# Sign-paired key features with 65-column key-value products, and the last 96 gate and up columns computed token-major and turned by a crossbar transpose

## The chip, the cores and the metric

The kernel runs on one NeuronCore of a Trainium2 chip (trn2). The metric is the device time of one execution in microseconds (us), the median of several. "Idle" always means idle time of TensorE unless another engine is named. The span of a profile is about 1.7 us shorter than the time of the same execution; both are given where they are used, and not mixed.

## The reference, cut to what matters

The input has S = 2048 tokens of D = 512 values. Two blocks, a linear attention (A) and a gated layer (B), run twice: A, B, A, B. In what follows "first attention" and "second attention" are the two A blocks, B1 and B3 the two gated layers.

```python
def A(x, wqkv, w_phi, wo):                    # 32 heads of 16
    q, k, v = split(x @ wqkv)                 # per head
    pq, pk = q @ w_phi, k @ w_phi             # per head, 16x16
    phi_q = concat([softmax(pq), softmax(-pq)])   # two signs of 16 features
    phi_k = concat([softmax(pk), softmax(-pk)])
    kv  = einsum("bhsf,bhsd->bhfd", phi_k, v) # sum over all 2048 tokens
    z   = einsum("bhsf->bhf", phi_k)
    num = phi_q @ kv ;  den = phi_q @ z + 1e-6
    return concat_heads(num / den) @ wo

def B(x, W_gate, W_up, W_down):               # F = 1376 = 10*128 + 96
    return (relu(x @ W_gate) * (x @ W_up)) @ W_down

x = x + A(layernorm(x)); x = x + B(layernorm(x))
x = x + A(layernorm(x)); x = x + B(layernorm(x))
```

## The kernel before, the parts that matter

The program is a list of operations, each with what it reads and writes, a declared duration and a name. A list scheduler inside the kernel orders them per engine from the declared durations, before anything runs. So a change of one operation changes the order of all.

`phik` scales the exponentials of the keys by their row sums (the softmax). `kv_acc` adds one token tile to the key-value sums: 8 products per tile, 16 tiles, each the 128 features of eight heads of one sign against the 128 values of the same eight heads. Only the eight diagonal blocks of 16x16 are wanted, so 7/8 of each product is thrown away. One more column, the 129th, is all ones and gives z. `kv_fin` masks the diagonal blocks out of PSUM into `kvbd`, a bank at a time, and `num` multiplies it with the queries' features.

```python
def knorm(self, t, tag):          # softmax of the key features of tile t
    op("dve", ... tensor_reduce(Zk, expk[:, t] as (s h) x 16), ...)           # row sums
    op("dve", ... reciprocal(rZk, Zk), ...)
    parts = [("pool", 0, 2)] if t < NT - 2 else [("pool", 0, 1), ("dve", 1, 2)]
    for eng, s0, s1 in parts:
        op(eng, ... tensor_tensor(expk, expk, rZk broadcast, ALU.mult), ..., f"{tag} phik {t} {s0}")

def kv_acc(self, t, tag):
    for g in range(NG):                                # 8 groups: 2 signs x 4 blocks of 8 heads
        s, c = g // 4, g % 4
        bank, j = g // 3, g % 3                        # three PSUM banks
        op("pe", ... matmul(pb[bank][:, j*130 : j*130+129],
                            expk[:, t, s, c*128:(c+1)*128], vsb[:, t, c, 0:129],
                            start=(t == 0 and j == 0), stop=(t == NT-1)),
           [r("phik", t, s), r("v", t), r("vones")], [RP[bank]], 59, f"{tag} kvacc {t} {g}")

def kv_fin(self, tag):
    for bank in range(3):                              # waits for ONE bank
        op("dve", ... tensor_tensor(kvbd[:, g0:g0+n, 0:128], pv[:, :, 0:128], mask8, ALU.mult),
           [RP[bank], r("mask8")], [r("kvbd", bank)], ...)
        op("dve", ... scalar_tensor_tensor(kvbd[:, g0:g0+n, 128:136], pv[:, :, 128:129], ...), ...)

def num(self, t, ...):                                 # needs kvbd of its bank only
    op("pe", ... matmul(pb[bank], expq[...], kvbd[:, g0 + j, :]), [r("expq", ...), r("kvbd", gb), ...], ...)
    # ... evacuate, divide, then a crossbar transpose of the result and the product with wo:
    dma_tr(... dma_start_transpose(oT[:, ob], osb[:, b]), ..., f"{tag} otr {t}")

def glu_up(self, ts, ...):                             # 128 rows of F at a time, feature-major
    def step(fc):
        Mf = 128 if fc < 10 else FLAST                 # FLAST = 96
        for bank, W in ((gb, Wg), (ub, Wu)):
            for ic in range(4):
                op("pe", ... matmul(pb[bank][0:Mf, 0:n], W[:, ic, fc*128 : fc*128+Mf], yT[:, ic, c0:c0+n]), ...)
        # relu on ACT, product on DVE into hT
```

In most stages the layer norm's result reaches TensorE through a crossbar transpose too, `tr t`, from `ytile` to `yT`.

The softmax here doesn't subtract the row's maximum and nothing guards it: scores larger than these inputs give would overflow.

Of the kernel before, what the change touches and what calls it, by code (L numbers as in the profile page):

```python
# [347 lines left out]
ALU = mybir.AluOpType  # L348
ACT = mybir.ActivationFunctionType
AX = mybir.AxisListType  # L350
P = 128

S, D, H, DH, F = 2048, 512, 32, 16, 1376
# [5 lines left out]
EPS_LN = 1e-5  # L359
EPS_DEN = 1e-6  # L360

WINDOW = {"sp": 24, "act": 64, "pe": 400, "dve": 40, "pool": 24}
# [6 lines left out]
class Kernel:  # L369
# [27 lines left out]
    def alloc(self, E):  # L397
        nc = self.nc

        def sb(name, shape, dt=BF16):  # L400
            t = E(nc.sbuf_tensor(name, [P] + shape, dt))
            setattr(self, name, t)
            return t

        sb("x_sb", [NT, 512])
        sb("yT", [NC, S])
        sb("wv_p", [NC, 512])
        sb("Wqp", [NC, 512])
        sb("Wkp", [NC, 512])
        sb("wo_p", [NC, 512])  # L410
        sb("Wg", [NC, F])
        sb("Wu", [NC, F])
        sb("Wd", [NFC, 512])
        sb("expk", [NT, 2, 512])
        sb("vsb", [NT, NC, 130])
        sb("expq", [NSLAB, NC, 2, 512])
        sb("kvbd", [NG, GW])
        sb("hT", [NHU, 512])
        sb("numbf", [2, NG, GW])
        sb("tsc", [2, 1024])  # L420
        sb("osb", [2, 512])
        sb("oT", [4, NC, 128])
        sb("gate_sb", [3, 512])
        sb("ytile", [4, 512])
        sb("ident", [128])
        sb("mask8", [8])
        sb("mask8t", [8])
        sb("phi_c", [NC, DH])
        sb("stats6", [NT, 6], FP32)
        sb("mv", [NT, 2], FP32)  # L430
        sb("rv1", [NT, 1], FP32)
        sb("rstd", [NT, 1], FP32)
        sb("nmr", [NT, 1], FP32)
        sb("agg", [4, 3], FP32)
        sb("aggw", [2], FP32)
        sb("mhalf", [4, 1], FP32)
        sb("Zk", [2, 64], FP32)
        sb("rZk", [4, 64], FP32)
        sb("zm", [2, 64], FP32)
        sb("zd", [2, 32], FP32)  # L440
        sb("zr", [2, 32], FP32)
        sb("ab", [2, 64])
        self.ps = E(nc.psum_tensor("ps", [P, 8, 512], FP32))
        self.pb = [self.ps[:, i, :] for i in range(8)]
        self.RP = [self.r("pb", i) for i in range(8)]


    def setup(self):
# [47 lines left out]
        op("pool", lambda e: e.memset(k.aggw[:, 1:2], 1.0 / D), [], [r("aggw")], 100, "agg w1")  # L496
        op("pool", lambda e: e.memset(k.vsb[:, :, :, 128:130], 1.0), [], [r("vones")], 250, "v ones")
        op("pool", lambda e: e.tensor_copy(k.kvbd[:, :, 136:144], k.mask8[:].unsqueeze(1).to_broadcast([P, NG, 8])), [r("mask8")], [r("kvones")], 230, "kv ones")
# [113 lines left out]
    def kv_proj(self, t, ring, tag):  # L612
# [6 lines left out]
        for s in range(2):  # L619
            op("act", (lambda s: lambda e: e.activation(k.expk[:, t, s, :], k.pb[bk][:], ACT.Exp, scale=(1.0 - 2.0 * s)))(s),  # L620
               [self.RP[bk]], [r("expk", t, s)], 605, f"{tag} expk {t} {s}")
        op("act", lambda e: e.activation(k.vsb[:, t, :, 0:128], k.pb[bv][:].rearrange("p (c n) -> p c n", c=4), ACT.Copy),
           [self.RP[bv]], [r("v", t)], 600, f"{tag} vcopy {t}")
        self.knorm(t, tag)

    def knorm(self, t, tag):
        op, r, k = self.op, self.r, self
        zb, rb = t % 2, t % 4
        op("dve", lambda e: e.tensor_reduce(k.Zk[:, zb, :], k.expk[:, t, :, :].rearrange("p s (h f) -> p (s h) f", f=16), AX.X, ALU.add),  # L629
           [r("expk", t, 0), r("expk", t, 1)], [r("Zk", zb)], 1215, f"{tag} Zk {t}")  # L630
        op("dve", lambda e: e.reciprocal(k.rZk[:, rb, :], k.Zk[:, zb, :]), [r("Zk", zb)], [r("rZk", rb)], 545, f"{tag} rZk {t}")  # L631
        parts = [("pool", 0, 2)] if t < NT - 2 else [("pool", 0, 1), ("dve", 1, 2)]
        for eng, s0, s1 in parts:
            op(eng, (lambda s0, s1: lambda e: e.tensor_tensor(  # L634
                k.expk[:, t, s0:s1, :].rearrange("p s (h f) -> p (s h) f", f=16),
                k.expk[:, t, s0:s1, :].rearrange("p s (h f) -> p (s h) f", f=16),
                k.rZk[:, rb, s0 * 32:s1 * 32].unsqueeze(2).to_broadcast([P, (s1 - s0) * 32, 16]), ALU.mult))(s0, s1),
               [r("expk", t, s) for s in range(s0, s1)] + [r("rZk", rb)], [r("phik", t, s) for s in range(s0, s1)],
               (1930 if s1 - s0 == 2 else 980) if eng == "pool" else 1050, f"{tag} phik {t} {s0}")

    def kv_pair(self, t, ring, tag):
# [8 lines left out]
        for s in range(2):  # L650
            op("act", (lambda s: lambda e: e.activation(k.expk[:, t:t + 2, s, :], k.ps[:, kb[0]:kb[0] + 2, :], ACT.Exp, scale=(1.0 - 2.0 * s)))(s),
               [self.RP[b] for b in kb], [r("expk", tt, s) for tt in ts], 1030, f"{tag} expk {t} {s}")
        op("act", lambda e: e.activation(k.vsb[:, t:t + 2, :, 0:128], k.ps[:, vb[0]:vb[0] + 2, :].rearrange("p b (c n) -> p b c n", c=4), ACT.Copy),
           [self.RP[b] for b in vb], [r("v", tt) for tt in ts], 1030, f"{tag} vcopy {t}")
# [3 lines left out]
    def kv_acc(self, t, tag):  # L658
        op, r, k = self.op, self.r, self
        for g in range(NG):  # L660
            s, c = g // 4, g % 4
            bank, j = g // 3, g % 3
            op("pe", (lambda s, c, bank, j: lambda e: e.matmul(  # L663
                k.pb[bank][:, j * 130:j * 130 + 129], k.expk[:, t, s, c * 128:(c + 1) * 128], k.vsb[:, t, c, 0:129],
                start=(t == 0 and j == 0), stop=(t == NT - 1), skip_group_check=True))(s, c, bank, j),
               [r("phik", t, s), r("v", t), r("vones")], [self.RP[bank]], 59, f"{tag} kvacc {t} {g}")

    def kv_fin(self, tag):
        op, r, k = self.op, self.r, self
        for bank in range(3):  # L670
            g0 = bank * 3
            n = min(3, NG - g0)
            pv = k.pb[bank][:, 0:n * 130].rearrange("p (g m) -> p g m", m=130)
            op("dve", (lambda g0, n, pv: lambda e: e.tensor_tensor(
                k.kvbd[:, g0:g0 + n, 0:128].rearrange("p g (d h) -> p g d h", h=8),
                pv[:, :, 0:128].rearrange("p g (h d) -> p g d h", h=8),
                k.mask8[:].unsqueeze(1).unsqueeze(1).to_broadcast([P, n, 16, 8]), ALU.mult))(g0, n, pv),
               [self.RP[bank], r("mask8")], [r("kvbd", bank)], 550 if n == 3 else 430, f"{tag} kvbd {bank}")
            op("dve", (lambda g0, n, pv: lambda e: e.scalar_tensor_tensor(
                k.kvbd[:, g0:g0 + n, 128:136], pv[:, :, 128:129].to_broadcast([P, n, 8]), 0.5 * EPS_DEN,  # L680
                k.mask8[:].unsqueeze(1).to_broadcast([P, n, 8]), ALU.add, ALU.mult))(g0, n, pv),
               [self.RP[bank], r("mask8"), r("kvbd", bank)], [r("kvbd", bank)], 200, f"{tag} kvden {bank}")

# [12 lines left out]
    def num(self, t, nring, wring, tag):  # L696
# [3 lines left out]
        for gb in range(3):  # L700
# [3 lines left out]
            for j in range(n):  # L704
# [3 lines left out]
                    start=(j == 0), stop=True, skip_group_check=True))(s, c, j, g0, bank),  # L708
                   [r("expq", st, c, s), r("kvbd", gb), r("kvones")], [self.RP[bank]], 63, f"{tag} num {t} {g0 + j}")
            op("dve" if gb == 2 else "act", (lambda g0, n, bank: lambda e: evac(  # L710
# [32 lines left out]
    def glu_up(self, ts, ring, tag, out, on_act=()):  # L743
# [4 lines left out]
        def step(fc):  # L748
            Mf = 128 if fc < 10 else FLAST
            gb, ub = next(ring), next(ring)  # L750
# [11 lines left out]
            if fc in on_act:  # L762
                tu = 12 + u % 4
                ru = [r("expk", tu, 0), r("phik", tu, 0)]
                op("act", (lambda Mf, ub, tu: lambda e: e.activation(k.expk[0:Mf, tu, 0, 0:n], k.pb[ub][0:Mf, 0:n], ACT.Copy))(Mf, ub, tu),  # L765
                   [self.RP[ub]], ru, 170 + n * 0.833, f"{tag} up {ts[0]} {fc}")
                op("dve", (lambda Mf, tu, gs, u: lambda e: e.tensor_tensor(k.hT[0:Mf, u, 0:n], k.gate_sb[0:Mf, gs, 0:n], k.expk[0:Mf, tu, 0, 0:n], ALU.mult))(Mf, tu, gs, u),  # L767
                   [r("gate", gs)] + ru, [r("hT", u)], 150 + n * 0.535, f"{tag} h {ts[0]} {fc}")
# [3 lines left out]

        for fc in range(NFC):
            out.append(lambda fc=fc: step(fc))
# [22 lines left out]
    def emit(self):  # L797
# [6 lines left out]
        for t in tiles(0):  # L804
            self.ln(t, "L0", pe_bank=(7 if t < 2 else 6), copy_act=True)
        kr0, qr0 = cycle([4, 5, 6, 7]), cycle([3])
        def L(st):
# [164 lines left out]
```

## Time and profile before

| | before |
|---|---|
| time, median (range) | 392.27 us (391.47 to 392.65) in the runs taken beside the changed kernel |
| span of the profile, granted clock | 390.3 us, 1.000 |
| TensorE busy | 97% |
| matmul work at the streaming rate | 372.9 us (worked out below) |

The page of the kernel before opens with its span and the busy time of each engine, and its fourth part gives the shares of the chain of work that ended last:

```profile
span 390.3 us, 6397 instructions
PE 379.4 (97%) x2331; PEld 208.0 (53%) x2331; DVE 272.0 (70%) x547; ACT 206.6 (53%) x389; POOL 168.5 (43%) x284
...
PE 88%; POOL 4%; ACT 3%; DMA 2%; DVE 1%; issue 1%; ACTq 0%; POOLq 0%
```

The next lines are the table of windows of the kernel before: window in us, its length, then for each engine busy us and count, then the granted clock, the DMA share and GB/s.

```profile
24.00:54.00 30.00, 28.97 (x234) 16.86 (x233) 28.57 (x36) 22.89 (x33) 28.00 (x17) 1.00 0.56 166
54.00:72.00 18.00, 16.93 (x113) 8.87 (x110) 14.57 (x37) 16.59 (x24) 9.14 (x19) 1.00 0.37 92
72.00:152.00 80.00, 79.88 (x510) 47.48 (x511) 61.37 (x141) 32.92 (x76) 36.02 (x77) 1.00 0.23 44
238.00:258.00 20.00, 19.73 (x155) 11.37 (x153) 16.35 (x42) 16.03 (x25) 9.22 (x20) 1.00 0.20 41
```

At 24-54 us, where the first attention's products run, TensorE, DVE and POOL are all busy 93 to 97% of the time.

Busy time of a pipelined matmul says little: a 512-column matmul lasts 379 ns but the next starts 216 ns later. So I worked with the starts of the matmul records in the trace. Back to back they are 216 ns apart for 512 columns, 109 for 256, 63 for 144 and 56 for 129. The line through the first and the last of these (383 columns more cost 160 ns: 0.418 ns a column, 2.1 ns on top) gives 109 and 62 ns for the other two. Its sum over all matmuls, an estimate, is what I call *work* below (the 64 matmuls of 128 columns are counted on the line too, though in the trace they start 106 ns apart in the median); *idle* is the rest of the start-to-start time.

The costliest groups of the kernel before that the change touches, in the page's form (matmuls of the products, 96-column weight loads, weight loads of the products, masked copies): busy us, mean ns of one, then idle just before and what ended it.

```profile
L663 PE MATMUL ps<-vsb,expk 128*128 128x129 bf16 x256 | 19.9, 220 | 1.0 <-POOL expk L634 0.6 <-ACT expq L693 0.3
...
L758 PEld LDWEIGHTS ps<-yT,Wu 128*96 128x96 bf16 x40 | 4.8, 123 | 2.8
...
L663 PEld LDWEIGHTS ps<-vsb,expk 128*128 128x128 bf16 x256 | 17.0, 97 | 8.4 <-POOL expk L634 1.1 <-issue 1.0 <-ACT expq L693 0.5
...
L674 DVE TENSOR_TENSOR kvbd<-ps,mask 128x384 bf16<-128x384 f32 x4 | 2.1, 556 | 2.9 <-PE ps L663 2.9
```

### The profile page before, as it was taken

Reading aid. Unit: us, or ns where it says so; the run is one execution under the profiler, and the core shown is the slowest. Engines: PE = TensorE matmul, PEld = TensorE weight load, DVE = VectorE, ACT = ScalarE, POOL = GpSimd, SP = SyncE. Lnnn points to the kernel's source line nnn. Section 1 sums busy time; section 2 is a strip of 40 time slices with the busy share of each in tenths; the row PEclk is TensorE's granted clock in tenths of the full one; section 3 lists DMA queues with packets and bytes.
Section 4 is the critical chain, followed back from the end, with each engine's and each line's share of the span. In section 5 each row is a group of like instructions: output and inputs, shape, how many; then the busy total and the mean of one; then the engine's idle time right before and its main releaser. Section 6 shows DMA issues by size and latency. Waiting matters only on the chain.

```text
span 390.3 us, 6397 instructions
## 1 busy us (share of the span) xinstructions
PE 379.4 (97%) x2331; PEld 208.0 (53%) x2331; DVE 272.0 (70%) x547; ACT 206.6 (53%) x389; POOL 168.5 (43%) x284
## 2 busy tenths in 40 slices
PE   5999989999999999999999999999999999999997
PEld 3445554667644544444444457567774554444444
DVE  4999978877766888866766777897986776232222
ACT  5898859834633404533453484985563462553340
POOL 5499936641724363372244543584553242100000
DMA  6833682311311322401000110132323132100002
GB/s 179 228 67 71 191 299 53 69 40 32 53 40 27 43 55 44 84 10 28 14 15 0 27 29 3 40 80 57 55 55 69 27 42 67 29 14 27 17 12 67
DMA packets 61663, 23.01 MB, mean 59 GB/s; under 512 B 53472, under 2 KB 60608, under 8 KB 61632
## 3 DMA queue, kind: packets, MB, share of 16 engines
q1 hardware_dynamic: 60912, 22.02, 24.4%
q10 hardware_dynamic: 720, 0.59, 0.5%
q8 instruction: 18, 0.29, 0.3%
q14 instruction: 13, 0.11, 0.1%
HBM read 7.91 MB, written 2.10 MB: 26 GB/s over the span
## 4 chain that ended last, share of the span: by engine, by line
PE 88%; POOL 4%; ACT 3%; DMA 2%; DVE 1%; issue 1%; ACTq 0%; POOLq 0%
PE ps L758 39%; PE ps L785 19%; PE ps L617 7%; PE ps L737 7%; PE ps L690 6%; PE ps L706 4%; PE ps L663 3%; PE ps L648 2%; POOL expk L634 2%; ACT expq L693 2%; DVE stats L551 1%; DMA x_sb<-in_A_x_dram 1%; DMA hT<-in_A_wqkv_dram 1%; ACT expk L620 1%; POOL rstd L576 1%
## 5 line engine op out<-in xcount | busy, mean ns | idle before, releaser
L758 PE MATMUL ps<-yT,Wg 128*128 128x512 bf16 (+3 forms) x440 | 130.1, 337 | 0.5 <-DMA yT<-ytile 0.2
L758 PE MATMUL ps<-yT,Wu 128*128 128x512 bf16 (+3 forms) x440 | 129.6, 336 | 0.0
L760 ACT ACTIVATE gate_sb<-ps 128x512 bf16<-128x512 f32 (+3 forms) x110 | 55.9, 512 | 105.3 <-PE ps L758 102.9
L785 PE MATMUL ps<-Wd,hT 128*128 128x512 bf16 (+2 forms) x363 | 106.8, 373 | 0.0
L634 POOL TENSOR_TENSOR expk<-expk,rZk 128x1024 bf16<-128x1024 bf16 (+1 forms) x32 | 59.5, 1878 | 37.1 <-DVE rZk L631 19.7
L758 PEld LDWEIGHTS ps<-yT,Wg 128*128 128x128 bf16 (+1 forms) x440 | 43.4, 100 | 33.8 <-issue 1.1
L758 PEld LDWEIGHTS ps<-yT,Wu 128*128 128x128 bf16 (+1 forms) x440 | 43.7, 100 | 32.6 <-ACT expk L765 0.2
L767 DVE TENSOR_TENSOR hT<-gate_sb,expk 128x512 bf16<-128x512 bf16 (+3 forms) x73 | 29.8, 409 | 37.9 <-ACT expk L765 33.0
L785 PEld LDWEIGHTS ps<-Wd,hT 128*128 128x128 bf16 (+1 forms) x363 | 35.3, 98 | 36.6 <-DVE x_sb L787 0.6
L551 DVE BATCH_NORM_STATS2 stats<-x_sb 128x6 f32<-128x512 bf16 x64 | 42.6, 682 | 5.5 <-DMA x_sb<-in_A_x_dram 5.1
L366 ACT ACTIVATE numbf<-ps 128x432 bf16<-128x432 f32 x64 | 33.1, 536 | 19.5 <-PE ps L706 19.4
L629 DVE TENSOR_REDUCE Zk<-expk 128x64 f32<-128x1024 bf16 x32 | 37.7, 1194 | 5.7 <-ACT expk L620 5.4
L731 POOL TENSOR_TENSOR osb<-tsc 128x512 bf16<-128x512 bf16 x28 | 32.5, 1162 | 19.9 <-DVE tsc L726 17.8
L737 PE MATMUL ps<-wo_p,oT 128*128 128x512 bf16 x128 | 39.8, 379 | 0.0
L770 DVE TENSOR_TENSOR hT<-gate_sb,ps 128x512 bf16<-128x512 bf16 (+2 forms) x37 | 22.7, 613 | 20.8 <-PE ps L758 19.6
L693 ACT ACTIVATE expq<-ps 128x1024 bf16<-128x1024 f32 (+1 forms) x40 | 32.6, 861 | 7.3 <-PE ps L690 7.0
L765 ACT ACTIVATE expk<-ps 128x512 bf16<-128x512 f32 (+3 forms) x73 | 36.1, 497 | 0.1
L706 PE MATMUL ps<-kvbd,expq 128*128 128x144 bf16 x256 | 35.0, 226 | 0.5 <-ACT numbf L366 0.5
L620 ACT ACTIVATE expk<-ps 128x512 bf16<-128x512 f32 x44 | 23.9, 598 | 21.5 <-PE ps L617 21.2
L690 PE MATMUL ps<-yT,Wqp 128*128 128x512 bf16 x128 | 34.6, 379 | 0.6 <-ACT expq L693 0.5
L787 DVE TENSOR_TENSOR x_sb<-x_sb,ps 128x512 bf16<-128x512 bf16 (+1 forms) x33 | 22.0, 669 | 18.8 <-PE ps L785 18.4
L559 POOL TENSOR_TENSOR rstd<-rv,mhalf 128x1 f32<-128x1 f32 (+1 forms) x53 | 31.9, 607 | 2.9
(73 smaller groups left out, 429.2 us busy)
## 6 DMA issues: line engine op xcount, KB each, us to landing
out_dram<-x_sb SPq DMA_DIRECT2D x15, 128.0 KB, 1.7
x_sb<-in_A_x_dram SPq DMA_DIRECT2D x3, 512.0 KB, 6.2
Wu<-in_B_W_up_dram SPq DMA_DIRECT2D x4, 344.0 KB, 5.9
Wg<-in_B_W_gate_dram SPq DMA_DIRECT2D x4, 344.0 KB, 5.5
Wd<-in_B_W_down_dram SPq DMA_DIRECT2D x5, 256.0 KB, 6.9
yT<-ytile SPq DMA_TRANSPOSE x60, 2.5
hT<-in_A_wqkv_dram ACTq DMA_DIRECT2D x4, 128.0 KB, 3.1
x_sb<-in_A_x_dram SPq DMA_DIRECT2D x4, 128.0 KB, 3.7
```

Of the source, the lines that this page charges most:

```text
L366: return e.activation(out, in_, ACT.Copy) if hasattr(e, "activation") else e.tensor_copy(out, in_)
L551: op("dve", (lambda t: lambda e: e.bn_stats(k.stats6[:, t, :], k.x_sb[:, t, :]))(t), [r("x", t)], [r("st", t)], 685, f"{tag} stats {t}")
L629: op("dve", lambda e: e.tensor_reduce(k.Zk[:, zb, :], k.expk[:, t, :, :].rearrange("p s (h f) -> p (s h) f", f=16), AX.X, ALU.add), [r("ex ...
L634: op(eng, (lambda s0, s1: lambda e: e.tensor_tensor(k.expk[:, t, s0:s1, :].rearrange("p s (h f) -> p (s h) f", f=16), k.expk[:, t, s0:s1, ...
L690: op("pe", (lambda c, ic, bank: lambda e: e.matmul(k.pb[bank][:], k.Wqp[:, ic, c * 128:(c + 1) * 128], k.yT[:, ic, st * 512:(st + 1) * 512 ...
L693: op("act", (lambda c0, s, b0: lambda e: e.activation(k.expq[:, st, c0:c0 + w, s, :], k.ps[:, b0:b0 + w, :], ACT.Exp, scale=(1.0 - 2.0 * s ...
L706: op("pe", (lambda s, c, j, g0, bank: lambda e: e.matmul(k.pb[bank][:, j * GW:(j + 1) * GW], k.expq[:, st, c, s, tt * 128:(tt + 1) * 128], ...
L737: op("pe", (lambda c, bank: lambda e: e.matmul(k.pb[bank][:], k.oT[:, ob, c, :], k.wo_p[:, c, :], start=(c == 0), stop=(c == NC - 1)))(c, ...
L758: op("pe", (lambda bank, W, ic, fc, Mf: lambda e: e.matmul(k.pb[bank][0:Mf, 0:n], W[:, ic, fc * 128:fc * 128 + Mf], k.yT[:, ic, c0:c0 + n] ...
L760: op("act", (lambda Mf, gb, gs: lambda e: e.activation(k.gate_sb[0:Mf, gs, 0:n], k.pb[gb][0:Mf, 0:n], ACT.Relu))(Mf, gb, gs), [self.RP[gb] ...
L765: op("act", (lambda Mf, ub, tu: lambda e: e.activation(k.expk[0:Mf, tu, 0, 0:n], k.pb[ub][0:Mf, 0:n], ACT.Copy))(Mf, ub, tu), [self.RP[ub] ...
L785: op("pe", (lambda fc, Kf, u, c0, bank, m0, m1: lambda e: e.matmul(k.pb[bank][:, m0:m1], k.hT[0:Kf, u, c0:c0 + 128], k.Wd[0:Kf, fc, m0:m1] ...
```

## The change

Two independent parts.

1. *Sign-paired features.* The key features are stored so that the 64 features of four heads of one sign lie beside the 64 of the other sign. One product then takes both signs of four heads against the 64 values of those heads and a ones column: 65 columns instead of 129, the same number of products (256), two PSUM banks instead of three. The finish must now pull 64x256 blocks out of both banks: 8 DVE operations. The query projections of the first attention get the free bank.
2. *Token-major tail of gate and up.* The last 96 of the 1376 columns were 48 matmuls of 512 columns and 32 of 256, using 96 of 128 output rows. Now gate and up together are one 192-column operand with tokens as rows: 128 matmuls of 192 columns. The result is token-major, so 10 crossbar transposes (`htr`) turn it back.

```diff
@@ kv_acc
-            s, c = g // 4, g % 4
-            bank, j = g // 3, g % 3
-                k.pb[bank][:, j * 130:j * 130 + 129], k.expk[:, t, s, c * 128:(c + 1) * 128], k.vsb[:, t, c, 0:129],
-                start=(t == 0 and j == 0), stop=(t == NT - 1), skip_group_check=True))(s, c, bank, j),
-               [r("phik", t, s), r("v", t), r("vones")], [self.RP[bank]], 59, f"{tag} kvacc {t} {g}")
+            bank, col = g // 4, (g % 4 // 2) * 256 + (g % 2) * 66
+                k.pb[bank][:, col:col + 65], k.expk[:, t, g, :, :].rearrange("p s m -> p (s m)"), k.vsb[:, t, g, 0:65],
+                start=(t == 0 and g % 4 == 0), stop=(t == NT - 1), skip_group_check=True))(g, bank, col),
+               [r("phik", t, bank), r("v", t), r("vones")], [self.RP[bank]], KVD, f"{tag} kvacc {t} {g}")
@@ kv_fin
-        for bank in range(3):                      # [cut] 2 operations per bank, reading that bank
+        for s in range(2):
+            for u in range(2):
+                src = k.ps[s * 64:s * 64 + 64, 0:2, :]...[:, :, u * 66:u * 66 + 65]
+                dst = k.kvbd[u * 64:u * 64 + 64, s * 4:s * 4 + 4, :]
+                op("dve", ... tensor_tensor(dst[..., 0:128 strided], src[:, :, 0:64], mask4, ALU.mult),
+                   [self.RP[0], self.RP[1], r("mask4")], [r("kvbd", s, u)], 420, f"{tag} kvbd {s} {u}")
+                op("dve", ... scalar_tensor_tensor(dst[:, :, 128 + u * 4:132 + u * 4], src[:, :, 64:65], ...),
+                   [self.RP[0], self.RP[1], ...], [r("kvbd", s, u)], 200, f"{tag} kvden {s} {u}")
@@ glu_up
-            Mf = 128 if fc < 10 else FLAST
+            Mf = 128
+        def last():
+            for j, t in enumerate(ts):
+                for ic in range(NC):
+                    op("pe", ... matmul(pv[:, j, 0:2 * FLAST], k.yT[:, ic, t * 128:(t + 1) * 128],
+                                        k.Wgu[:, ic, :, F - FLAST:F]), ..., 84, f"{tag} gu {t} {fc} {ic}")
+            # [cut] relu on ACT, product on DVE, into h10t
+            self.dma_tr(... dma_start_transpose(hT[:, u, 0:n], h10t[:, 0:m, :]), ..., f"{tag} htr {ts[0]}")
+        out.append(last)                           # first step of each group of tiles
-        for fc in range(NFC):
+        for fc in range(NFC - 1):
```

(Cut: the storage of `expk`, `vsb` and `kvbd` with their memsets, `mask4`, and `qr0 = cycle([2, 3])` in place of `cycle([3])`. `KVD = 40.0` is the duration declared to the scheduler.)

## The prediction

> **What bounds the kernel now.** TensorE's streaming rate. The page gives PE 97% busy at granted clock 1.000; busy time alone proves little, because a 512-column matmul lasts 379 ns but starts 216 ns after the one before. So I took start-to-start distances of the matmul records in the trace: 216 ns (N=512), 109 (256), 63 (144), 56 (129, the key-value products). [...] Summed over the 2331 matmuls it makes 372.9 us; the rest is 2.6 us before the first matmul and about 12 us of stalls: 5.7 in the first 20 us, some 4 at 20-72 us, 1.5 at 240-260, almost none elsewhere. The chain of waits agrees: PE 88%, POOL 4%.
>
> **Removed from PE.**
> 1. Gate/up, last 96 columns: 48 matmuls at 216 and 32 at 109 ns = 13.9 us become 128 of 192 columns at 82.5 ns [...] = 10.6 us. Gain 3.3 us, all in stages with no stall: kept in full.
> 2. Key-value products: 256 matmuls, 129 columns to 65, which took 15.3 us by start-to-start. By streaming alone they would need 29.6 ns each (7.6 us). They may instead hit a floor of weight loads, one per matmul: nothing in this trace goes under 55 ns. Loads of 128 columns last 97 ns, of 96 columns 123 ns; [...] and estimate 36 ns per matmul (30 to 45). Gain 5.5 us on PE, half in each attention. In the second attention PE is the limit: kept, 2.7 us. In the first, DVE and POOL are both busy 13.0 of 13 us at 28-41 us (table of windows), POOL's key scaling (1.93 us a tile) paces the products until 51 us; only filler work (query projections, which get bank 2 back, as the products now fill two banks) turns the saving into time. I count 1.9 us.
>
> **Added.** Ten crossbar transposes (2.5 us each to landing, as the existing 92), issued first in each stage and needed last: hidden. The key-value finish becomes 8 DVE operations of about 0.42 and 0.18 us instead of 6: 2.4 against 2.1 us, and the first numerators need four of them instead of two; some 0.5 us later twice, mostly covered by query projections. Two memsets on POOL lie in early idle time. One stall goes: query projections waiting for the single bank 3 at 49-52 us (1.2 us); I count 0.5. A new schedule is worth about 1 us either way.
>
> **Sum.** 392.3 - 3.3 - 2.7 - 1.9 - 0.5 + 0.3 = 384.2 us, 2.1% faster. 8 in 10: 380.8 to 388.0. Faster by over 2%: 0.52; within 2%: 0.46; slower: 0.02.
>
> **What would show each step.** 192-column matmuls 82-84 ns apart and no 96-column weight loads; runs of key-value products 30-45 ns apart; the second attention's tail (237-240 us) shorter by over 1 us; PE stall at 20-72 us not up by more than 1 us; no PE wait on the new transposes.
>
> **What would make it wrong.** A weight-load floor near 55 ns (gain only 4 us: about 388); POOL pacing the first attention so that nothing is kept there (386); or no floor and fewer stalls around the first attention (381).

The sum came to 384.2 us, and all its terms stand above. The 372.9 us is the sum over the line (0.418 ns a column, 2.1 on top), and the 82.5 and 29.6 ns are estimates that lie within 0.4 ns of that line. The 36 ns is the estimate, between the 29.6 and the 56 ns measured for 129 columns; on it rest the gain of 5.5 us and the terms 2.7 and 1.9.

## More of the kernel before

The timeline of the kernel before at the end of the second attention's products (start us, us, engine, line, operation, then idle before it and what ended it):

```profile
237.22 2.77 PE L663 MATMUL ps<-vsb,expk 128*128 128x129 bf16 x45
...
238.70 1.08 DVE L674 TENSOR_TENSOR kvbd<-ps,mask 128x384 bf16<-128x384 f32 x2 [1.43 <-PE ps L663]
239.70 0.30 DVE L679 SCALAR_TENSOR_TENSOR kvbd<-ps,mask 128x24 bf16<-128x24 f32 x2
239.83 0.38 PE L690 MATMUL ps<-yT,Wqp 128*128 128x512 bf16 x1
...
240.04 0.54 PE L706 MATMUL ps<-kvbd,expq 128*128 128x144 bf16 x6
```

The first masked copies (L674) start at 238.70, while the last 45 products (L663) still run: the finish works per bank. TensorE goes from the last product to a query projection (L690) and on to the numerators (L706).

## The result, and the profile after

| | before | after |
|---|---|---|
| time, median (range) | 392.27 us (391.47 to 392.65) | 396.52 us (396.05 to 397.8) |
| ratio, 95% interval | | 1.0112 [1.0091, 1.0134] |
| span of the profile, clock | 390.3 us, 1.000 | 394.3 us, 0.996 |
| work of TensorE | 372.9 us | 362.7 us |

Every ratio in this document is the mean time of one kernel's fast runs over the mean of the other's in the same rounds, so it is not quite the ratio of the medians quoted. The interval is clear: the kernel became 1.1% slower, and the prediction of 384.2 us (380.8 to 388.0) missed. TensorE has 10.1 us less to do and the kernel takes 4 us longer.

The page of the kernel after: span, engines, the queue of instruction packets (packets, MB, share), and the chain that ended last.

```profile
span 394.3 us, 6478 instructions
PE 373.5 (95%) x2379; PEld 203.8 (52%) x2379; DVE 273.6 (69%) x551; ACT 203.2 (52%) x381; POOL 172.5 (44%) x287
...
q8 instruction: 19, 0.31, 0.4%
...
PE 78%; POOL 9%; DVE 7%; DMA 3%; issue 2%; ACT 1%; SPq 0%; POOLq 0%; DVEq 0%
```

PE's share of the chain fell from 88 to 78%. POOL went from 4 to 9 and DVE from 1 to 7: a part of the limit has moved to those two. The table of windows of the kernel after, with one row more for the start of B3:

```profile
24.00:54.00 30.00, 27.06 (x233) 14.20 (x234) 27.89 (x35) 23.61 (x34) 28.49 (x17) 1.00 0.46 128
54.00:72.00 18.00, 15.88 (x112) 8.37 (x110) 14.39 (x38) 14.80 (x23) 6.78 (x15) 1.00 0.43 134
72.00:152.00 80.00, 78.77 (x529) 47.97 (x528) 62.19 (x140) 32.35 (x74) 38.18 (x80) 1.00 0.27 52
238.00:258.00 20.00, 17.26 (x130) 9.17 (x127) 15.42 (x40) 16.59 (x25) 7.77 (x16) 1.00 0.12 25
258.00:268.00 10.00, 7.31 (x53) 5.76 (x54) 6.24 (x17) 5.43 (x14) 6.01 (x14) 0.83 0.41 65
```

B1's stretch (72-152) is nearly as full as before. The loss is at 24-72 and at 238-268. At 24-54 POOL is now 95% busy while TensorE waits. At 238-258 TensorE does 130 matmuls where it did 155. At 258-268 the granted clock is 0.83: part of that window ran at half clock.

The groups of the kernel after that answer to those shown before:

```profile
L668 PE MATMUL ps<-vsb,expk 128*128 128x65 bf16 x256 | 12.7, 193 | 0.4 <-POOL expk L642 0.3
...
L668 PEld LDWEIGHTS ps<-vsb,expk 128*128 128x128 bf16 x256 | 11.5, 97 | 6.5 <-POOL expk L642 0.7 <-ACT vsb L628 0.3
...
L790 PE MATMUL ps<-Wgu,yT 128*128 128x192 bf16 x128 | 16.2, 251 | 2.3 <-DMA yT<-ytile 2.3
...
L680 DVE TENSOR_TENSOR kvbd<-ps,mask 64x256 bf16<-64x256 f32 x8 | 3.4, 422 | 3.5 <-PE ps L668 3.3
...
L685 DVE SCALAR_TENSOR_TENSOR kvbd<-ps,mask 64x16 bf16<-64x16 f32 x8 | 1.4, 172 | 0.2
```

The operations themselves cost what was expected or less. Back to back the 65-column products start 29 ns apart and the 192-column ones 82 to 83, both on the line of the kernel before (29.3 and 82.3); the finish's DVE times are 422 and 172 ns against the 0.42 and 0.18 us of the prediction. So the new operations are not slow. The waits around them are.

The timeline of the kernel after, at the end of the second attention's products:

```profile
239.60 0.41 PE L668 MATMUL ps<-vsb,expk 128*128 128x65 bf16 x8
...
240.07 1.32 DVE L680 TENSOR_TENSOR kvbd<-ps,mask 64x256 bf16<-64x256 f32 x3 [2.00 <-PE ps L668]
241.43 0.36 DVE L685 SCALAR_TENSOR_TENSOR kvbd<-ps,mask 64x16 bf16<-64x16 f32 x2
...
241.85 0.42 PE L712 MATMUL ps<-kvbd,expq 128*128 128x144 bf16 x4 [1.84 <-DVE kvbd L685]
```

The last products (L668) are no earlier than before. The first masked copy (L680) starts at 240.07, after the last product, and not 1.1 us before it. TensorE has nothing else ready and stands still for 1.84 us.

The list of TensorE's waits after (line, what it waited for: us in total, times, longest):

```profile
PE ps L712 <- DVE kvbd L685: 3.5, 3, 1.8
...
PE ps L790 <- DMA yT<-ytile: 2.3, 2, 1.8
PE ps L654 <- DMA yT<-ytile: 2.3, 2, 2.0
PE ps L743 <- DMA oT<-osb: 2.0, 3, 1.1
```

And the one line of the same list before that comes nearest to these:

```profile
PE ps L758 <- DMA yT<-ytile: 0.2, 1, 0.2
```

Waits for the finish (kvbd) are new, and those for crossbar transposes of *old* tensors (yT, oT) were at most 0.2 us before. There is no wait on one of the new transposes (hT<-h10t) anywhere. The DMA part of the page gives those a median of 2.4 us from issue to landing:

```profile
hT<-h10t SPq DMA_TRANSPOSE x10, 2.4
```

Where the idle time is can be seen by cutting the execution at milestones of TensorE's own program. Worked out from the matmul starts, in us (single rows are rounded):

```
idle TensorE                              before    after    more
start to first product, attention 1         6.0      7.5     1.5
first to last product, attention 1          1.9      4.2     2.4
last product to first numerator             0.1      0.9     0.8
to the first gate/up of B1                  1.9      2.6     0.7
to the last product of attention 2 (B1)     0.3      1.6     1.4
last product to first numerator, att. 2     0.0      2.0     2.0
to the first gate/up of B3                  0.8      4.4     3.6
rest (B3)                                   0.6      1.8     1.3
sum                                        11.5     25.1    13.6
work                                      372.9    362.7   -10.1
```

13.6 - 10.1 = 3.5 us, about the 4 us by which the span grew. The task of the experiments is to say why the saved work turned into idle time.

### The profile page after: what moved, and what is told of

It reads as the page before. It is cut to its first block, busy times and chain, and to the rows that moved or that the text cites. A ratio compares the mean times of both kernels' runs of the same rounds, so it can differ in the third digit from the quotient of the medians.

```text
span 394.3 us, 6478 instructions
## 1 busy us (share of the span) xinstructions
PE 373.5 (95%) x2379; PEld 203.8 (52%) x2379; DVE 273.6 (69%) x551; ACT 203.2 (52%) x381; POOL 172.5 (44%) x287
## 4 chain that ended last, share of the span: by engine, by line
PE 78%; POOL 9%; DVE 7%; DMA 3%; issue 2%; ACT 1%; SPq 0%; POOLq 0%; DVEq 0%
PE ps L764 35%; PE ps L813 19%; PE ps L623 8%; POOL expk L642 6%; PE ps L743 6%; PE ps L712 3%; PE ps L790 3%; PE ps L696 3%; DMA oT<-osb 1%; DVE stats L557 1%; DMA x_sb<-in_A_x_dram 1%; PE ps L668 1%; DMA yT<-ytile 1%; DVE kvbd L680 1%; DVE Zk L635 1%
## 5 line engine op out<-in xcount | busy, mean ns | idle before, releaser
L764 PE MATMUL ps<-yT,Wgu 128*128 128x512 bf16 (+1 forms) x800 | 176.2, 338 | 0.0
L764 PEld LDWEIGHTS ps<-yT,Wgu 128*128 128x128 bf16 x800 | 77.8, 99 | 60.5 <-ACT gate_sb L766 0.6
L813 PE MATMUL ps<-Wd,hT 128*128 128x512 bf16 (+2 forms) x363 | 104.2, 373 | 0.0
L766 ACT ACTIVATE gate_sb<-ps 128x512 bf16<-128x512 f32 (+1 forms) x100 | 50.9, 513 | 84.0 <-PE ps L764 80.6
L774 DVE TENSOR_TENSOR hT<-gate_sb,expk 128x512 bf16<-128x512 bf16 (+1 forms) x65 | 27.3, 426 | 32.4 <-ACT expk L772 29.8
L743 PE MATMUL ps<-wo_p,oT 128*128 128x512 bf16 x128 | 39.2, 379 | 2.2 <-DMA oT<-osb 2.0
L815 DVE TENSOR_TENSOR x_sb<-x_sb,ps 128x512 bf16<-128x512 bf16 (+1 forms) x33 | 21.9, 666 | 24.3 <-PE ps L813 24.3
L564 POOL TENSOR_SCALAR rv<-mv 128x1 f32<-128x1 f32 (+1 forms) x53 | 12.5, 244 | 55.9 <-DVE mv L559 55.8
L712 PE MATMUL ps<-kvbd,expq 128*128 128x144 bf16 x256 | 32.7, 228 | 3.5 <-DVE kvbd L685 3.5
L772 ACT ACTIVATE expk<-ps 128x512 bf16<-128x512 f32 (+1 forms) x65 | 32.2, 499 | 0.5 <-PE ps L764 0.5
L600 DVE TENSOR_SCALAR ytile<-x_sb,mv,rstd 128x512 bf16<-128x512 bf16 x52 | 26.3, 512 | 7.2 <-POOL rstd L565 7.2
L623 PE MATMUL ps<-Wkp,yT 128*128 128x512 bf16 x88 | 29.7, 390 | 1.0 <-ACT yT L611 0.8
```

The lines of the kernel that those rows point to most:

```text
L623: op("pe", (lambda ic, bank, W: lambda e: e.matmul(k.pb[bank][:], k.yT[:, ic, t * 128:(t + 1) * 128], W[:, ic, :], start=(ic == 0), stop=( ...
L712: op("pe", (lambda s, c, j, g0, bank: lambda e: e.matmul(k.pb[bank][:, j * GW:(j + 1) * GW], k.expq[:, st, c, s, tt * 128:(tt + 1) * 128], ...
L743: op("pe", (lambda c, bank: lambda e: e.matmul(k.pb[bank][:], k.oT[:, ob, c, :], k.wo_p[:, c, :], start=(c == 0), stop=(c == NC - 1)))(c, ...
L764: op("pe", (lambda bank, W, ic, fc, Mf: lambda e: e.matmul(k.pb[bank][0:Mf, 0:n], W[:, ic, fc * 128:fc * 128 + Mf], k.yT[:, ic, c0:c0 + n] ...
L766: op("act", (lambda Mf, gb, gs: lambda e: e.activation(k.gate_sb[0:Mf, gs, 0:n], k.pb[gb][0:Mf, 0:n], ACT.Relu))(Mf, gb, gs), [self.RP[gb] ...
L813: op("pe", (lambda fc, Kf, u, c0, bank, m0, m1: lambda e: e.matmul(k.pb[bank][:, m0:m1], k.hT[0:Kf, u, c0:c0 + 128], k.Wd[0:Kf, fc, m0:m1] ...
```

## The experiments

### The two halves alone

e1 takes the key-value half of the change only, e2 the gate/up half only.

```diff
 # e1: all hunks of the change but glu_up's      # e2: only glu_up's, with h10t and Wgu
```

> The key-value half of the change alone (sign-paired features, 65-column products, new finish), gate and up as before. Theory (attention stages are paced by the chain softmax - finish - numerators on DVE, POOL, ACT and DMA, so TensorE time saved there turns into idle time, and the new finish lengthens the chain): 394 to 398 us, products 29 ns apart, idle TensorE up by 8 us or more against before. Rival (the crossbar transposes of the other half cost the time): 386 to 388 us.

> The gate/up half alone (192-column products and crossbar transpose), attention as before. Theory: the full 3.3 us of TensorE time are kept, 388 to 389 us, no wait of TensorE on the new transposes. Rival (transposes hold up the shared queue): 392 us or more, with waits on yT, oT or hT in the gate/up stages.

Measured: e1 395.99 us, ratio 1.0117 [1.010, 1.0134]. e2 389.62 us, ratio 0.9951 [0.9936, 0.9966]. The gate/up half gains 1.9 us, the key-value half alone is as slow as the whole change. The second is what neither the prediction nor its own list of dangers had. In e1's trace TensorE stands idle for 1.6 and 2.0 us before the first numerators of the two attentions. e2's trace has no wait on the new transposes, but 1.5 us before B3's second tile, on an old one.

### Is shorter product work worth anything?

e3 keeps the kernel before and its exact order of instructions. It only makes each product 65 columns wide. The result is wrong: the finish, with as many elements as before, reads eight of the written columns over and over.

```diff
-   k.pb[bank][:, j * 130:j * 130 + 129], k.expk[...], k.vsb[:, t, c, 0:129],
+   k.pb[bank][:, j * 130 + 64:j * 130 + 129], k.expk[...], k.vsb[:, t, c, 64:129],
@@ kv_fin
-   pv[:, :, 0:128].rearrange("p g (h d) -> p g d h", h=8),
+   pv[:, :, 64:72].unsqueeze(2).to_broadcast([P, n, 16, 8]),
```

> The kernel before with products of 65 instead of 129 columns, and nothing else: same instructions, same order on every engine, same finish (which reads written columns only). Results wrong on purpose. TensorE work falls by 6.8 us. If TensorE's streaming bounds the attention stages, as I predicted, or if only the new order is to blame, the time falls by 5 to 7 us, to 386 us. If the chain through DVE and POOL paces them, it falls by 1 to 2.5 us, to about 390.5, and the rest appears as idle time of TensorE before products and numerators.

Measured: 391.67 us, ratio 0.9999 [0.9984, 1.0014]. TensorE has 6.8 us less work (256 times 64 columns at the 0.418 ns a column of the kernel before) and the time does not move. A part of the 6.8 us is found in the view of the products' line, what was waited for before them, first in e3 (the sum of the waits of the matmuls and of their weight loads, which overlap):

```profile
L663 PE MATMUL ps<-vsb,expk x256: 190/193/203, 24.0 to 238.2; 128*128 128x65 bf16 x128
...
  POOL expk L634: 6.6, 9
```

and in the kernel before:

```profile
L663 PE MATMUL ps<-vsb,expk x256: 217/220/231, 24.5 to 239.8; 128*128 128x129 bf16 x128
...
  POOL expk L634: 1.7, 3
```

The sum of both is 6.6 us for POOL's scaling of the keys instead of 1.7; the matmuls alone wait 3.6 us instead of 0.6, of which 2.4 us lie in the first attention (0.6 before) and 1.1 in the second (none before). In the kernel before, the products were long enough to hide the softmax that feeds them. Shortening them uncovers it. Another 1.0 us of e3 is chance: a late transpose (4.83 us from issue to landing) for which TensorE waits, of the kind that is explained further below.

### Does the saving come back when the softmax is light?

e11 lightens the softmax in the kernel before: row sums and scaling touch 2 of each 16 elements (wrong; the comparison with the reference does not notice, for a reason that was not looked into). e12 is e11 with 65-column products as in e3.

```diff
 # e11, in knorm: the three views of expk
-   ...rearrange("p s (h f) -> p (s h) f", f=16)
+   ...rearrange("p s (h f) -> p (s h) f", f=16)[:, :, 0:2]
 # e12: the same, and e3's edit
```

> The kernel before, same instructions and order, with the key softmax's row sums (DVE, 1.2 us a tile) and scaling (POOL, 1.9 us) shrunk to an eighth of their elements. Results wrong on purpose. TensorE streaming as before at 129 columns, so little is to be won: 389.5 to 391.5 us in either theory. It is the partner of the next run.

> The same with 65-column products: the narrow run (which gained nothing: 391.7) with a light key softmax. If the softmax on DVE and POOL is what paced the products: now 3 to 6.5 us less than its partner, 384 to 388 us. If the products' saving is lost elsewhere (order, numerators, transposes): within 1.5 us of its partner.

Measured: e11 390.78 us, ratio 0.9959 [0.9939, 0.9978]; e12 387.27 us, ratio 0.987 [0.9849, 0.9891]. The same narrowing that was worth nothing is worth 3.5 us once the softmax is light. The view of the products' line in e12 shows the wait on POOL gone:

```profile
L663 PE MATMUL ps<-vsb,expk x256: 191/193/204, 23.7 to 233.6; 128*128 128x65 bf16 x128
...
  ACT vsb L622: 0.2, 1
```

So it is shown that the softmax on DVE and POOL paced the products of the kernel before, once they were narrow. It isn't the whole pace: 3.5 of 6.8 us came back, not 6.8, and some 0.5 of the 3.5 may be chance (TensorE waits 0.7 us for a late transpose in e11, 0.2 in e12). What holds the rest was not taken apart. Nor does a run show how much of this acts in the kernel after. There the matmuls of the products wait only 0.3 us for POOL; the waits of the first attention fall before the key projections instead, on transposes of `yT`, while DVE and POOL are busy 93 and 95% of the time (24-54 us).

### What does the new finish cost?

e4 is the kernel after with the masked copies shrunk from 256 to 16 elements a row (wrong), in the same order. e8 is a right kernel: the whole change, but each head's 16 values get their ones column behind them (17 x 4 = 68 columns), so that one masked copy of 64x272 brings the numerator and the denominator, and the finish is 4 operations instead of 8.

```diff
 # e4
-   src[:, :, 0:64].rearrange("p c (h d) -> p c d h", h=4),
+   src[:, :, 0:64].rearrange("p c (h d) -> p c d h", h=4)[:, :, 0:1, :],
 # e8
-        sb("vsb", [NT, NG, 66])
+        sb("vsb", [NT, NG, 68])          # 4 heads x (16 values + one)
-   dst[:, :, 0:128]... src[:, :, 0:64]... [64, 4, 16, 4]      and a second operation for the denominators
+   dst[:, :, 0:136]... src[:, :, 0:68]... [64, 4, 17, 4]      and no second operation
 # [cut] two small buffers of the division share storage with other tiles
```

> The kernel after with the same instructions in the same order, but the four masked copies of the finish shrunk from 256 to 16 elements a partition. Results wrong on purpose. If the finish on DVE lengthens the chain: about 1.2 us less between last product and first numerator in each attention, the clock dip after the second one gone, 392 to 394.5 us in all. If the finish is hidden: within 0.5 us of after (396.5).

> The kernel after with a shorter, correct finish: a column of ones behind each head's 16 value columns (68-column products), so that one operation of 272 elements does the masked copy and the denominators together: 4 operations instead of 8, and the first numerators need 2. New order, so instruction packets fall elsewhere. If the finish lengthens the chain: last product to first numerator 0.8 to 1.3 us instead of 2.0 in the second attention, and 393 to 395 us in all, less if the packets miss the transposes. If the finish is hidden: 396 or more.

Measured: e4 394.22 us, ratio 1.0071 [1.0046, 1.0097]; e8 394.47 us, ratio 1.0053 [1.0018, 1.0087]. In the second attention the idle time between the last product and the first numerator went from 2.0 to 1.3 us in e4 and 1.2 in e8. Part of the gain was lost later in both: in each, another transpose (`otr 3`, the attention's output of tile 3) came late, and TensorE waited 2.9 and 2.8 us for it. In time the two can't be told from chance: a repeat of the kernel after itself (e5, below) gave 1.0062. So the shorter wait is shown, a gain in time is not. The late transposes pointed at the next suspect.

### Late transposes, and the instruction packets

In the kernel after, TensorE waited 2.2 us at 41 us for the transposed tile 12, and 2.0 us at 261 us for B3's first tile. Both transposes took 4.0 and 4.1 us from issue to landing, not the usual 2.4. But the trace also lists the core's own instruction packets of 16 KB. The page counts 19 of them after and 18 before, and 255 TensorE records lie between one and the next in the median of both traces (210 to 312; 4758 matmuls and weight loads in all after). That they go with TensorE's program is seen in e9 below: 80 more TensorE instructions in front moved the two packets named next 4.9 and 5.6 us earlier. Packets of the kernel after start at 39.5 and 258.6 us, on top of exactly these two transposes (issued at 37.6 and 257.6). Times here are those of the profile's views; the expectations count from some 0.3 us later, so that their 39.2 and 258.3 us are the same packets. Over 16 profiled executions (all but those of e5 and e7), for all crossbar transposes issued after 62 us:

```
                                                      landed after, median   over 2.9 us
a packet starts within 2.4 us after the issue (168)         3.71 us             80%
  of these, 0.25 to 2.0 us after it (116)                   3.79 us            100%
none (1177)                                                 2.42 us              5%
```

The bounds 0.25 and 2.0 were chosen after looking. The stretch before B3 can be seen in the timeline. SyncE's transposes and TensorE in the kernel after (SPq is SyncE's queue; its durations are those of the queue's records, and the landing is seen in TensorE's wait):

```profile
257.57 3.54 SPq L603 DMA_TRANSPOSE yT<-ytile  x2
...
258.86 1.04 PE L743 MATMUL ps<-wo_p,oT 128*128 128x512 bf16 x4 [1.06 <-DMA oT<-osb]
...
261.73 0.61 PE L790 MATMUL ps<-Wgu,yT 128*128 128x192 bf16 x4 [1.83 <-DMA yT<-ytile]
```

and the same pair of transposes of the kernel before:

```profile
254.02 2.50 SPq L597 DMA_TRANSPOSE yT<-ytile  x2
```

Before, the pair takes 2.50 us in the queue; after, 3.54, and B3 cannot start until it has landed.

To test it, the packets have to be moved in time without a change of anything else: put some instructions in front of TensorE's program. The first try used empty instructions (e5: 72 before the kernel after, e6: 56 before the kernel before, e7: 96 before e2).

```diff
+        for _ in range(72 if e == "pe" else 0):      # e5; e6: 56, e7: 96
+            eng.nop()
```

> The kernel after with 72 no-operations ahead of TensorE's program, nothing else. In its profile 16 KB packets of the instruction queue, about one for every 256 TensorE instructions, overlap crossbar transposes that TensorE waits for (of token tile 12 at 37-41 us, of the second attention at 256-261 us); transposes so overlapped land after 3 to 4.5 us instead of 2.4. The no-operations move every later packet some 5 us earlier, off these. If the collisions cost the time: 391.5 to 394.5 us, idle before the products of tile 12 and before the second gate/up stage down by 1 us or more each. If not: within 0.7 us of after, 396.5 or a little more.

> The kernel before with 56 no-operations ahead of TensorE's program: this moves instruction packets onto the transposes of tile 12 (32-35 us) and of the first two tiles of the first gate/up stage (67-71 us), which the kernel before escapes. If the collisions cost time: slower by 0.8 to 3 us, 392.5 to 394.7 us, with new TensorE idle time there. If not: 391.7 us, within 0.5.

> The gate/up half alone with 96 no-operations ahead. Alone it kept 2.0 of 3.3 us; its profile shows 1.5 us of idle TensorE at 257 us before the second token tile of the second gate/up stage, whose transpose an instruction packet overlaps. If that is the reason: 387.8 to 388.8 us. If the transposes themselves or their queue are: 389.6 us.

This failed: the build dropped the empty instructions and the packets stayed where they were. So the three are only repeats: e5 395.06 us, ratio 1.0062 [1.0037, 1.0087]; e6 391.59, 0.9983 [0.9959, 1.0006]; e7 390.42, 0.9948 [0.9925, 0.9971]. They are useful as a measure of chance: the same kernel after gave 1.0112 and 1.0062. So differences of half a per cent between different runs of the kernel after say little. The first executions of e5 and e7 took 2221.8 and 1409.6 us, the former with gate and up matmuls of 1441 ns in the mean (338 in the kernel after) at a reported clock of 1.0. They are left out; I cannot explain them.

The second try used real work: constant 16-column matmuls into a bank not yet in use, in front of TensorE's program, while it waits for the first data anyway.

```diff
+        if e == "pe":
+            ones = self.kernel.tsc[:, 0, 0:128]
+            eng.wait_ge(sems["pool"], <count after the constant is set>)
+            for _ in range(40):                      # e9: 40, e10: 44, e13: 48, e14: 40
+                eng.matmul(self.kernel.pb[7][:, 0:16], ones, ones[:, 0:16], start=True, stop=True)
```

e9 is the kernel after with 40 of these, e10 the kernel before with 44, e13 the gate/up half (e2) with 48.

> The no-operations of the shift runs never reached the program, so those runs were repeats. This is the kernel after with 40 real 16-column matmuls of constants ahead of TensorE's program, in its idle first 3 us (80 instructions with their weight loads). If instruction packets on crossbar transposes cost the time: packets some 5 us earlier than 39.2 and 258.3 us, no idle of 2 us before the products of tile 12 nor before the second gate/up stage, no clock dip there, 391 to 394 us. If not: 395 to 397 us with the same idle stretches. [...]

> The kernel before with 44 such matmuls ahead: this puts an instruction packet on the transposes of the first two tiles of the second gate/up stage (253 to 257 us), which it escapes without. If packets cost time: idle TensorE of 1 us or more at 256 to 260 us, 392.5 to 394.5 us[...]. If not: 391 to 392 us.

> The gate/up half alone with 48 constant matmuls ahead, which move the instruction packet at 254.7 us off the transpose of the second gate/up stage. If packets cost there: 1 to 1.5 us less than alone (0.995 of before): 387.8 to 389 us, 0.990 to 0.993 of before. If not: 0.995.

Measured, e9: 392.69 us, ratio 1.0016 [0.9988, 1.0045], correct. Against the kernel before it is level, where the kernel after stood at 1.0062 and 1.0112: 2 to 4 us gained (the interval of e9 just overlaps that of the 1.0062, [1.0037, 1.0087]). The packets moved to 34.6 and 253.0 us; the idle time before tile 12 fell from 2.2 to 0.65 us (tile 14 now waited 1.3), and before B3's first tile from 2.0 to 0.4. The timeline of e9 there:

```profile
258.47 2.58 SPq L609 DMA_TRANSPOSE yT<-ytile  x2
...
261.02 0.50 PE L796 MATMUL ps<-Wgu,yT 128*128 128x192 bf16 x4 [0.23 <-DMA yT<-ytile]
...
262.33 0.50 PE L796 MATMUL ps<-Wgu,yT 128*128 128x192 bf16 x4 [0.50 <-DMA yT<-ytile]
```

The pair is back at 2.58 us. The profiled execution is e9's slowest (394.36; the three others 391.9 to 392.9), because it had half clock at 57.0 us (see below).

e13: 388.12 us, ratio 0.9903 [0.9888, 0.9918], correct; its span is 386.2 us at clock 1.000. The idle time before B3's second tile went from 1.5 us to none. Its interval lies apart from those of e2 and its repeat e7. This is the best right kernel and beats both.

e10: 392.62 us, ratio 1.0008 [0.9984, 1.0031]. The expected slowdown of the kernel before did not come, and the trace shows why: the packet at 254.1 us started 1.6 us before the first of the two B3 transposes was issued (255.7), and these took the usual 2.5 us. Another packet, at 146.4 us, started 2.0 us after the issue of a transpose in B1, which took 4.5 us, and TensorE waited 1.2 us for it. So the total supports neither side on the packets, and the one hit that it had fits. Another reading of e9 and e13 is that the extra matmuls gain time by themselves, for instance by an earlier start of the products. The traces speak against it: the first product starts at 24.9 us in e9 as in the kernel after, and at 24.3 us in e13 against 24.2 in e2.

### The half clock

In the profile of the kernel after, the clock is 0.5 from 262.0 us for 3.4 us, right after the 2.0 us of idle time. If TensorE is the limit there, half of 3.4 is lost, 1.7 us (an estimate from these two numbers). The same was seen in e1, e4, e8, e9 and e16. No single long gap stood before it in e9 (two of 0.9 and 1.1 us): what the eight cases in the traces have in common is that TensorE was idle for 2.1 to 2.9 us in sum in the 3.4 us before. Not every wait of that size was followed by one: the 2.0 us of e9 at 240.7 us were not. By arithmetic one such stretch in 394 us makes a mean clock of 0.996, two make 0.991. The four executions of the kernel after had 0.996 once and 0.991 three times; the 32 executions of the kernel before whose clock is on record all had 0.999 or more.

How much it costs is mixed in the times. In e8 the execution at clock 1.000 took 392.65 us, three at about 0.996 took 393.62 to 394.48, the one at 0.991 took 396.57. In e9 the one at 0.994 took 394.36 and the three at 1.000 took 392.4 in the mean. But in e16 the execution at 1.000 (396.61) is no faster than two at 0.996 (396.41 and 396.83), and in e5 it is the same. But two kept traces isolate it. The kernel after and e9 run the same instructions in the same order. From the first numerator of the first attention to the first gate/up of B1 the kernel after, at full clock, takes 17.16 us; e9, with half clock from 57.0 us and nearly the same waits, takes 18.81: 1.65 us more. So half clock for 3.4 us cost nearly all of the 1.7 us there. In these traces it came after waits like those above and added its own cost to theirs.

### Both remedies, and the rival readings

e14 puts the remedies together: the whole change, the 4-operation finish of e8, 40 leading matmuls. e15 and e16 test whether it was only the order: e15 is e8 with declared durations set to measured ones and the best plan of some hundreds of perturbed orders (its edit shows only the one chosen); e16 is the kernel after with the products' declared duration set to 29.6 ns instead of 40.

```diff
 # e15, on top of e8
+            jitter = random.Random(463)
+            prio = [weight * o.idx - rank[o.idx] - o.boost + jitter.gauss(0, 500.0) for o in ops]
 # (and declared durations of rstd, apply, DMA and KVD set to the measured)
 # e16
-KVD = 40.0
+KVD = 29.6
```

> The whole change with the 4-operation finish and 40 constant matmuls ahead. In its profile without them a packet at 256.1 us hits a transpose, TensorE idles 2.8 us and its clock halves for 3.4 us. If packets and finish were both real terms: 389.5 to 391.5 us, faster than before by 0.2 to 0.6%. If only order is to blame: 394 as without.

> The whole change with the 4-operation finish, the durations in the list scheduler set to those of the traces (31 ns per product, 0.75 us for a layer norm on DVE in the first stage, and so on), and the best of some 200 perturbed orders by the kernel's own replay. If order was the cause of the missing gain: 386 to 389 us. If the chain is: no better than 390.

> The kernel after with the duration of a product given to the list scheduler as the measured 29.6 ns instead of 40: same instructions, another order. If the wrong duration spoiled the order: 390 to 393 us. If not: within 1.5 us of after, 395 to 396.5 us.

Measured: e14 390.72 us, ratio 0.9971 [0.9956, 0.9985], correct; e15 392.43, 1.0008 [0.9991, 1.0026]; e16 396.83, 1.0121 [1.0104, 1.0137]. A wrong declared duration is not the cause (e16). Another order does not make the whole change win either (e15), so the rival theory "the scheduler drew a bad order" can't be the whole cause. It may be a part: e15 stands 0.4% below e8 (the intervals overlap), with packets elsewhere too, and that search covers some orders, not all. With both remedies the whole change beats the kernel before by 0.3%. Between e8 and e14 only the 40 leading matmuls differ, and the ratio falls from 1.0053 to 0.9971, with intervals apart: in the profiles the wait of 2.8 us falls to 0.9 and the half clock after it is gone. This is the clearest case for the packets.

The timeline of e14 at the end of the second attention's products shows what the remedy does and does not do:

```profile
237.25 1.85 DVE L686 TENSOR_TENSOR kvbd<-ps,mask 64x272 bf16<-64x272 f32 x4 [2.02 <-PE ps L674]
...
238.20 0.42 PE L714 MATMUL ps<-kvbd,expq 128*128 128x144 bf16 x4 [1.02 <-DVE kvbd L686]
```

The wait is 1.02 instead of 1.84 us. It stays above zero: the copies still read both banks and start after the last product. No run tried a finish per bank.

And yet the gate/up half alone (e13) is faster than the mended whole (e14) by 2.6 us (medians). The table by milestones says where:

```
idle TensorE                              before   after    e13    e14
first to last product, attention 1          1.9     4.2     1.6    4.2
last product to first numerator, att. 2     0.0     2.0     0.0    1.2
first numerator to gate/up of B3            0.8     4.4     0.6    2.3
rest (B3)                                   0.6     1.8     0.3    1.6
all, with the stretches not shown          11.5    25.1    10.3   18.8
work                                      372.9   362.7   369.6  363.1
```

e14 has 6.5 us less work than e13 and 8.5 us more idle time: the time that shorter products save is eaten by idle time, much of it in and just after the stretches where it was saved.

## Why the prediction was wrong, point by point

- *"TensorE's streaming rate" bounds the kernel: right for B1 and B3, wrong for the attentions.* In the gated layers the removed work was kept. In the attentions a chain of softmax (DVE, POOL), products, finish (DVE), numerators and transposes was about as long as TensorE's program. For the softmax e3 and e12 show it; for the rest it is read from the waits. TensorE at 97% busy showed little slack, but the other engines had little either (DVE 95%, POOL 93% at 24-54 us).
- *Gate/up, 3.3 us "kept in full": right in size once the packets are out of the way.* e2 kept 1.9 us, e13 3.7 us. The new transposes are hidden, as predicted: 2.4 us, no wait on hT<-h10t in any list.
- *The products' time: better than predicted.* 36 ns each was estimated, with 30 to 45 as range; they start 29 ns apart. The feared floor from weight loads did not show, though each product has its own load of 97 ns.
- *"In the second attention PE is the limit: kept, 2.7 us": this is the step that failed,* and with it the 1.9 us counted for the first attention. e3 kept 0 of 6.8 us. e12 shows a part of the reason, with 3.5 us back when the softmax was made light. In the kernel after itself the time went another way: the products of the second attention hardly wait, but 24 matmuls of its query projections run before the last product, where 16 did before, so that it starts at 239.8 us in both kernels; then these projections are missing when TensorE waits for the finish (2.0 us) and the transposes (3.6 us more idle time up to B3). I had read a stage in which TensorE is busy all the time as one in which TensorE alone decides. The predicted sign of it, a tail shorter by over 1 us, was right to look for, and it did not come.
- *The finish: "some 0.5 us later twice, mostly covered by query projections": mis-sized.* In the whole change TensorE stands idle 0.8 us longer in the first and 2.0 us longer in the second attention. I had counted four operations against two. What matters more is that each new copy reads both banks, so none can start while products still run, where before the first one started 1.1 us before the last product; and that no query projection was ready to cover it. That it is the reading of both banks is argued from the timelines. e4 and e8 take 0.7 to 0.8 us of the idle time back.
- *Waits on old transposes: not foreseen.* Packets of instructions delayed two transposes on the critical path by about 1.6 us each (4.0 and 4.1 us to landing, not 2.4). Some 2 us of idle time followed each time, and in the profile once a half clock after it, which cost about 1.65 us where two traces isolate it. e9 moved the packets and gained 2 to 4 us against the kernel after (ratio 1.0016 against 1.0062 and 1.0112). This is a chance property of where the packets fall, not of the change's idea; the change adds 48 matmuls, and its packets start at other times (39.5 and 258.6 us, where the kernel before has 37.1 and 261.5).
- *The bank that the query projections get back, 0.5 us:* no run isolates it.

What stays open: why the stretch from the second attention's numerators to B3 keeps 2.3 us of idle time even in e14, why a packet delays a transpose at all, what holds back the other half of the narrowing in e12, and the two very slow executions.

## What to carry to other kernels

When several engines are each busy nearly all of a stage (here 93 to 97% at 24-54 us), cutting one of them may buy nothing until the next one gives way (e3: 0 of 6.8 us; e12: 3.5): before counting a saving, make that one operation narrower in the unchanged order, even with a wrong result, and see whether the time moves (e3 would have warned of the whole key-value half). When a reduction is finished in pieces, keep the pieces independent: with the finish that reads both banks, TensorE stood idle for 2.0 us between the last product and the first numerator of the second attention, where the finish per bank left 0.0. And when a small unrelated change moves the time by a per cent, look where the instruction packets fall against the critical transposes before believing either a gain or a loss (here 3.71 us to landing in the median with a packet within 2.4 us after the issue, 2.42 without).
